# Two attention pairs project keys and queries in split form, and raw inputs share two buffers

## The chip, the cores and the metric

The kernel runs on one core of one Trainium2 chip. The metric is the device time of one execution in microseconds. A profiled execution is recorded by the hardware profiler; its trace gives every instruction with its start and duration.

## The reference

Three stages run one after the other, all in float32.

- Linear attention for 4 batches of 8 heads, 576 positions, head size 64. For queries and keys, `proj = x @ w_phi` (64 to 128 features), the row's largest absolute value is taken off, and the features are `[exp(proj), exp(-proj)]`. Then `kv = k_p^T v`, `z = sum(k_p)`, and the output is `(q_p kv) / (q_p z + 1e-6)`.
- A maxout layer on 2304 tokens: `h = max(x w1, x w2, x w3)`, 512 to 768, followed by `h @ w_out` back to 512.
- A layer with learned slopes: `h = x w_in` (512 to 2048), `g = max(h, 0) + alpha * min(h, 0)`, then `g @ w_out`.

## The kernel before

**Pairs.** Heads are taken in pairs, 16 in all (4 batches of 4 pairs), numbered here from 0. A pair's 576 positions are four tiles of 128 and a tail of 64; the tails of its keys and its queries share one fifth tile. So each pair has nine projections of one tile: four of keys, four of queries, one of tails. `project` (line 204) does two tiles in one PSUM bank of tag `pj`, which has two buffers; VectorE then reduces the bank to row maxima (line 212) and, for most uses, adds them back (`less_max`, line 216).

**Two forms of a product.** In the plain form a projection is one float32 matmul of 128x256. In the split form `features` (line 192) makes two reduced-width halves of the raw tile on VectorE, a cast (line 67, tiles `xh..`) and a subtraction (line 70, tiles `xl..`), and three matmuls of 128x256 take the products high by high, high by low and low by high, with the weights' halves `wph` and `wpl`. Pairs 0 to 4 are plain (`PLAIN = 5`), pairs 5 to 15 are split. The halves of keys and queries have two buffers of tag `xh` and two of tag `xl`.

**Loads.** `load_pair` (line 140) loads keys `k`, tails `t`, queries `q` and values `v` on SyncE's queue. In plain pairs the raw keys lie in the two buffers of tag `xh` and the raw queries in the two of `xl`. In split pairs raw keys and raw queries take turns in two buffers of tag `raw`. The tails have one buffer.

**The loop** (line 453). For pair i it emits the loads of pair i+1, then `queries` of pair i-1 interleaved with `keys` of pair i, then the conversion of some weight tiles of the maxout layer (`CONVERT_IN`, of lowest priority), and from pair 5 on some units of the maxout layer (`layer1`), which are other TensorE work beside the attention. The halves `wph` and `wpl` are emitted just before the keys of pair 4.

**What sets the order.** The code is written as above, but a planner with a model of the engines' times sorts each engine's instructions, and the loads of SyncE's queue, by priority and by when their inputs and buffers are ready. The order is then fixed: each engine and each queue goes through its list in order, and waits on semaphores. The keys of batch 0 have neutral priority; queries of the pair before have a slightly lower one, weight conversions a still lower one.

Of the kernel before, what the change touches and what calls it, by code (L numbers as in the profile page):

```python
# [38 lines left out]
XBUFS = 6  # L39
LAG = 2  # L40
KEYS_ONLY = ("rv", "rt", "vh", "vl", "e", "kh", "kl", "my", "begun", "xht", "xlt")
PLAIN = 5
CONVERT_IN = (0, 1, 1, 2, 2, 3, 4, 5)
SOON, NOW, LATER, LAST = 400, 1000, -100, -200

# [2 lines left out]
def tile_kernel(ctx: ExitStack, tc: tile.TileContext, qT, kT, tails, v, w_phi, w1, w2, w3, w_out, w_in, w_out2, alpha, out):  # L48
# [14 lines left out]
    def hi_act(dst, src):  # L63
        A.activation(dst, src, AF.Copy)  # L64

    def hi_dve(dst, src):
        V.tensor_copy(dst, src)

    def sub(eng, dst, src, hi):
        eng.tensor_tensor(dst, src, hi.bitcast(F32), op=ALU.subtract)  # L70
# [18 lines left out]
    def run(*steps):  # L89

        steps = list(steps)
        while steps:
            for x in list(steps):
                if next(x, x) is x:
                    steps.remove(x)
# [13 lines left out]
    def bank(tag, bufs, nm):  # L109
        return ps.tile([P, 512], F32, tag=tag, bufs=bufs, name=nm)  # L110
# [8 lines left out]
    def at(shape, dtype, name, tag=None, bufs=1):  # L119
        pool = ap if (tag or name) in KEYS_ONLY else lp  # L120
        return pool.tile(shape, dtype, name=name, tag=tag or name, bufs=bufs)
# [18 lines left out]
    def load_pair(pair):  # L140

        odd = pair[1] % 2
        tags = ["xh", "rv", "rt", "xl"] if plain(pair) else ["raw", "rv", "rt", "raw"]
        if plain_kv(pair):
            tags[1] = ("vl", "vh")[odd]
        shapes = ([P, SM], [P, 5, 3, D], [P, 2 * ST], [P, SM])
        for what, tag, shape, src in sorted(zip("kvtq", tags, shapes, (kT, v, tails, qT)), key=lambda x: ("ktqv" if i_of(pair) else "ktvq").index(x[0])):
            t = at(shape, F32, tag=tag, bufs=2 if tag in ("raw", "xh", "xl") else 1, name=what)
            for part in (slice(0, 2 * P), slice(2 * P, SM)) if what == "k" and i_of(pair) == 0 else (slice(None),):
                nc.sync.dma_start(t[:, part], src[pair][:, part])  # L150
            raws[pair, what] = t

    def plain(pair):
        return i_of(pair) < PLAIN

    def i_of(pair):
        return pair[0] * NPAIR + pair[1]

    def plain_kv(pair):
        return pair[0] < 2  # L160

    def split_w123(f, j):
        if j == 0:
            w.append([])
        t = ring.tile([P, 2, 512], F32R, tag="w", name="w123t")
        w[f].append(t)
        st = fetched.pop(0)
        wt = at([P, 512], F32, tag="kl", bufs=2, name="wt")
        yield from from_f64(st, wt, tc.keep_in_program_order, False)
        hi_act(t[:, 0], wt)  # L170
        yield
        sub(V, t[:, 1], wt, t[:, 0])
# [3 lines left out]
    def fetch(after):  # L176

        tag = ("kh", "qe")[len(unfetched) % 2]
        st = at([P, 1024], U32, tag=tag, bufs=2, name="wst")
        V.tensor_copy(st[:, :1].bitcast(F32), after[:, :1])  # L180
        nc.sync.dma_start(st, unfetched.pop(0).bitcast(U32))
        fetched.append(st)

    def at_priority(n, steps):
        while True:
            with tc.high_priority(offset=n):
                x = next(steps, steps)
            if x is steps:
                return
            yield  # L190
# [76 lines left out]
    def keys(pair):  # L267

        rv = raws[pair, "v"]
        if not plain_kv(pair):  # L270
            if not vs:
                vs.extend(at([P, 5, 3, D], F32R, tag=tag, bufs=1, name=tag) for tag in ("vh", "vl"))
                part = slice(None)
            else:
                part = slice(None, None, 2)
            vh, vl = vs
            hi_act(vh[:, :, part], rv[:, :, part])
            sub(V, vl[:, :, part], rv[:, :, part], vh[:, :, part])
        kvp = bank("kv", 1, "kvp")
        first = True  # L280
        for tiles, e in exp_keys(pair):
            n = len(tiles) * 512
            if not plain_kv(pair):
                kh = at([P, 1024], F32R, tag="kh", bufs=2, name="kh")
                kl = at([P, 1024], F32R, tag="kl", bufs=2, name="kl")
                hi_act(kh[:, :n], e[:, :n])
                sub(V, kl[:, :n], e[:, :n], kh[:, :n])
                ops = ((vh, kh), (vl, kh), (vh, kl))
            yield
            for i, t in enumerate(tiles if plain_kv(pair) else ()):  # L290
                for j in range(4):
                    c = slice(i * 512 + j * P, i * 512 + j * P + P)
                    nc.tensor.matmul(  # L293
                        kvp[:, j * P : (j + 1) * P],
                        e[:, c],
                        rv[:, t, j // 2 : j // 2 + 2].rearrange("p a d -> p (a d)"),
                        start=first,
                        stop=t == 4,
                        skip_group_check=True,
                    )  # L300
                    first = False
            for i, t in enumerate(() if plain_kv(pair) else tiles):
                for h in range(2):
                    c = slice(i * 512 + h * 256, i * 512 + h * 256 + 256)
                    for x, y in ops:
                        nc.tensor.matmul(  # L306
                            kvp[:, h * 256 : h * 256 + 256],
                            x[:, t, h : h + 2].rearrange("p a d -> p (a d)"),
                            y[:, c],
                            start=first,  # L310
                            stop=t == 4 and y is ops[-1][1],
                            skip_group_check=True,
                        )
                        first = False
        yield
        if plain_kv(pair):
            kvf = at([P, 2, 2, P], F32, tag=("kvh", "kvl")[pair[1] % 2], bufs=2, name="kvf")
            A.activation(kvf.rearrange("p a b c -> p (a b c)"), kvp, AF.Copy)  # L318
            kvs_of[pair] = (kvf,)
            return  # L320
        kvs = at([P, 512], F32, tag="kvs", bufs=1, name="kvs")
        A.activation(kvs, kvp, AF.Copy)
        kvt = bank("kv", 1, "kvt")
        for i in range(4):
            nc.tensor.transpose(kvt[:, i * P : (i + 1) * P], kvs[:, i * P : (i + 1) * P], ident)
        kvh = at([P, 2, 2, P], F32R, tag="kvh", bufs=2, name="kvh")
        kvl = at([P, 2, 2, P], F32R, tag="kvl", bufs=2, name="kvl")
        hi_act(kvh.rearrange("p a b c -> p (a b c)"), kvt)
        sub(V, kvl.rearrange("p a b c -> p (a b c)"), kvt, kvh.rearrange("p a b c -> p (a b c)"))
        kvs_of[pair] = (kvh, kvl)  # L330
# [114 lines left out]
    w = []  # L445

    load_pair(pairs[0])
    make_identity(nc, ident)
    al = const.tile([P, NF2], F32, name="al")
    nc.gpsimd.dma_start(al, alpha)  # L450
    G.tensor_scalar(al, al, -1.0, 1.0, op0=ALU.mult, op1=ALU.add)
    last = None
    for i, pair in enumerate(pairs):
        if i + 1 < len(pairs):
            load_pair(pairs[i + 1])
        with tc.high_priority(offset=(0, SOON, NOW, NOW)[pair[0]]):
            if i == PLAIN - 1:
                hi_dve(wph, wraw)
                sub(V, wpl, wraw, wph)
            run(*([at_priority(LATER, queries(last))] if last else []), keys(pair))  # L460
            last = pair
        count = CONVERT_IN[i] if i < len(CONVERT_IN) else 0
        for j in range(count):
            for _ in range(min(count, 4) if j == 0 else int(j + 3 < count)):
                fetch(begun[pair])
            with tc.high_priority(offset=LAST if i < NPAIR - 1 else 0):
                n = sum(len(x) for x in w)
                run(split_w123(n // 3, n % 3))
        u0 = 3 * (i - NPAIR) - LAG
        for u in range(u0, u0 + 3):  # L470
            if u >= 0:
                c, f = (u % 2, u // 2) if u < 12 else (u // NF1 % 2, u % NF1)
                layer1(u // 12, c, f, xs[u // 12], w[f])
# [369 lines left out]
    for block in range(nblocks):  # L843
        last = block == nblocks - 1
# [97 lines left out]
```

## Time and profile before

| what | us |
|---|---|
| median of 3 runs (lowest, highest) | 877.71 (877.59, 879.58) |
| the profiled execution's own time | 878.6 |
| its span, first to last instruction | 876.8 |
| TensorE matmuls busy | 868.5 |
| TensorE weight loads busy | 854.9 |
| VectorE busy | 637.3 |
| ScalarE busy | 514.5 |
| GpSimd busy | 158.4 |

Matmuls are pipelined, so the time between the ends of two of them, not the duration of one, is what one costs. Weight loads lie beside matmuls. Idle time of an engine that is not the bottleneck costs nothing.

### The profile page before, as it was taken

To read this page: it belongs to the slowest core of one execution; us is meant where nothing else is said; L and a number is where in the kernel's file an instruction comes from. 1 tells how busy PE (TensorE), PEld (TensorE's weight loads), DVE (VectorE), ACT (ScalarE), POOL (GpSimd) and SP (SyncE) were. 2 spreads that over 40 slices of the span, in tenths; PEclk is the share of its full clock that TensorE was granted. 3 is DMA by queue.
4 is the path that set the end of the run, shared out by engine and by line. 5 is a ranking of instruction groups with operands and counts; after the bars stand their busy time and mean duration, and the time that the engine had idled before them with its cause. 6 is when DMAs were issued, how large, how long until landed. Compare 5 with 4: busy or idle time off the path is not lost.

```text
span 876.8 us, 17441 instructions
## 1 busy us (share of the span) xinstructions
PE 868.5 (99%) x6631; PEld 854.9 (97%) x6631; DVE 637.3 (73%) x1196; ACT 514.5 (59%) x1055; POOL 158.4 (18%) x278
## 2 busy tenths in 40 slices
PE   9999999999999999999999999999999999999998
PEld 8888899999999999999999999999999999999998
DVE  5578878877888776683965754846478899988871
ACT  4666767777677765553853554646477763544440
POOL 0354222112322244211112301111111000000000
PEclk9999999999999999999999999999999999999999
DMA  6445653223332169661688863745348746433321
GB/s 234 140 157 161 180 154 113 76 86 85 88 89 70 36 215 349 212 208 35 195 266 309 314 230 134 225 182 189 123 136 265 268 158 202 150 125 121 120 74 49
DMA packets 70436, 142.99 MB, mean 163 GB/s; under 512 B 9152, under 2 KB 36176, under 8 KB 70352
## 3 DMA queue, kind: packets, MB, share of 16 engines
q1 hardware_dynamic: 53664, 92.95, 33.2%
q0 software_dynamic: 14816, 45.26, 15.0%
q10 hardware_dynamic: 1872, 3.67, 1.2%
q8 instruction: 52, 0.85, 0.4%
q14 instruction: 32, 0.26, 0.1%
HBM read 93.07 MB, written 46.34 MB: 159 GB/s over the span
## 4 chain that ended last, share of the span: by engine, by line
PE 82%; issue 8%; DMA 4%; ACT 3%; DVE 2%; POOL 1%; POOLq 0%; DVEq 0%; ACTq 0%
PE acc L861 20%; PE p L265 16%; PE sums L773 12%; PE pj L265 6%; PE pc L773 6%; PE pn L265 6%; PE kvp L293 4%; PE p L675 3%; PE kvp L306 3%; PE pb L773 3%; DMA st<-in_w_out 2%; PE pt L368 2%; DMA xr<-r_d 1%; DVE wt L86 1%; DMA st<-in_w_in 1%
## 5 line engine op out<-in xcount | busy, mean ns | idle before, releaser
L265 PE MATMUL p<-x,w123t 128*128 128x288 f32 x1728 | 251.4, 298 | 0.4 <-ACT s L436 0.4
L265 PEld LDWEIGHTS p<-x,w123t 128*128 128x128 f32 x1728 | 235.0, 188 | 2.3 <-ACT s L436 0.8
L773 PE MATMUL sums<-x,wi 128*128 128x288 f32 x768 | 107.7, 295 | 0.0
L861 PE MATMUL acc<-wq,o 128*128 128x256 f32 x864 | 105.5, 283 | 0.0
L861 PEld LDWEIGHTS acc<-wq,o 128*128 128x128 f32 x864 | 104.2, 189 | 0.0
L773 PEld LDWEIGHTS sums<-x,wi 128*128 128x128 f32 x768 | 104.0, 188 | 0.0
L861 PE MATMUL acc<-wq,x 128*128 128x256 f32 x648 | 78.1, 280 | 0.0
L675 PE MATMUL p<-x,wo 128*128 128x288 f32 x576 | 77.0, 296 | 0.6 <-ACT yo L679 0.6
L675 PEld LDWEIGHTS p<-x,wo 128*128 128x128 f32 x576 | 76.6, 188 | 0.9 <-ACT yo L679 0.8
L861 PEld LDWEIGHTS acc<-wq,x 128*128 128x128 f32 x648 | 77.0, 188 | 0.0
L792 DVE SCALAR_TENSOR_TENSOR g<-neg,al,g 128x576 f32<-128x576 f32 x64 | 50.3, 811 | 23.6 <-ACT neg L791 23.6
L212 DVE TENSOR_REDUCE mx<-pj 128x4 f32<-128x512 f32 (+1 forms) x80 | 50.1, 628 | 12.3 <-PE pj L265 12.2
L781 ACT ACTIVATE s<-sums 128x576 f32<-128x576 f32 x48 | 31.1, 647 | 42.0 <-PE sums L773 41.9
L77 ACT ACTIVATE wt<-st 128x512 f16<-128x512 bf16 x38 | 30.1, 799 | 42.5 <-DVE wt L514 14.0
L793 POOL DMA_DIRECT2D g_d<-g x32 | 22.9, 715 | 167.2 <-DVE g L792 165.4
L441 POOL DMA_DIRECT2D h_d<-ho x48 | 28.2, 587 | 137.8 <-DVE ho L439 116.3
L245 ACT ACTIVATE ke<-pj,mx 128x128 f32<-128x128 f32 x96 | 36.9, 384 | 14.7 <-DVE mx L212 14.5
L293 PEld LDWEIGHTS kvp<-v,ke 128*128 128x128 f32 x320 | 40.6, 191 | 4.7 <-ACT kvf L318 1.8
L293 PE MATMUL kvp<-v,ke 128*128 128x128 f32 x320 | 42.9, 278 | 1.6 <-ACT kvf L318 1.6
L791 ACT ACTIVATE neg<-g 128x576 f32<-128x576 f32 x64 | 40.2, 675 | 6.3 <-DVE g L823 5.9
L64 ACT ACTIVATE o<-wt 128x512 fp32r<-128x512 f32 x45 | 27.4, 627 | 24.7 <-PE acc L861 14.2
L400 POOL DMA_DIRECT2D xr<-r_d x64 | 34.1, 539 | 32.3 <-DMA r_d<-dc 21.6
(161 smaller groups left out, 1779.6 us busy)
## 6 DMA issues: line engine op xcount, KB each, us to landing
g_d<-g POOLq DMA_DIRECT2D x32, 576.0 KB, 3.6
a<-g_d SPq DMA_DIRECT2D x36, 512.0 KB, 4.3
st<-in_w_out SPq DMA_DIRECT2D x22, 512.0 KB, 5.8
wst<-in_w SPq DMA_DIRECT2D x18, 512.0 KB, 4.0
st<-in_w_in SPq DMA_DIRECT2D x16, 512.0 KB, 4.7
yr<-y_d SPq DMA_DIRECT2D x28, 288.0 KB, 3.9
v<-in_v SPq DMA_DIRECT2D x16, 480.0 KB, 4.4
q_d<-wt POOLq DMA_DIRECT2D x28, 256.0 KB, 5.3
```

The lines of the kernel that those rows point to most:

```text
L77: order(A.activation(half[:, :, 1].bitcast(F16), lanes[:, :, 3].bitcast(BF16), AF.Copy))
L212: V.tensor_reduce(mx, pv, axis=AX.X, op=ALU.max, apply_absolute_value=True, negate=True)
L245: A.activation(ev[:, a, 0], pv[:, a], AF.Exp, bias=mx[:, a : a + 1])
L265: nc.tensor.matmul(dst, x, y, start=i == 0, stop=i == len(ops) - 1, **kw)
L293: nc.tensor.matmul(kvp[:, j * P : (j + 1) * P], e[:, c], rv[:, t, j // 2 : j // 2 + 2].rearrange("p a d -> p (a d)"), start=first, stop=t ...
L400: nc.gpsimd.dma_start(xr[r], rows[h : h + 1, cs].to_broadcast([D, CH]))
L675: nc.tensor.matmul(p2[m // 2][1][:, m % 2], x, y, start=k + n == 0, stop=k == NF1 - 1 and n == 2)
L773: nc.tensor.matmul(dst[:, j], a, b, start=start and n == 0, stop=n == len(ops) - 1, skip_group_check=True)
L781: A.activation(s, src, AF.Copy)
L791: A.activation(neg, gv[:, j], AF.Relu, scale=-1.0)
L792: V.scalar_tensor_tensor(gv[:, j], neg, al[:, f + j : f + j + 1], gv[:, j], op0=ALU.mult, op1=ALU.add)
L861: nc.tensor.matmul(acc[i], x, y, start=half == 0 and f == 0 and n == 0 and place[i][1] == 0, stop=half == 1 and f == 3 and n == 2, skip_gr ...
```

## The change

Plain are now pairs 0, 3 and 4 alone; pairs 1 and 2 use the split form. The raw keys and queries of every pair but the first lie in the two buffers of tag `raw`, also those of the plain pairs 3 and 4, which therefore keep such a buffer until their last projection has read it. The halves of the weights are emitted after the keys of pair 0.

```diff
-PLAIN = 5
+PLAIN = (0, 3, 4)
...
     def load_pair(pair):
 
         odd = pair[1] % 2
-        tags = ["xh", "rv", "rt", "xl"] if plain(pair) else ["raw", "rv", "rt", "raw"]
+        tags = ["xh", "rv", "rt", "xl"] if i_of(pair) == 0 else ["raw", "rv", "rt", "raw"]
...
     def plain(pair):
-        return i_of(pair) < PLAIN
+        return i_of(pair) in PLAIN
...
         with tc.high_priority(offset=(0, SOON, NOW, NOW)[pair[0]]):
-            if i == PLAIN - 1:
+            run(*([at_priority(LATER, queries(last))] if last else []), keys(pair))
+            if i == 0:
                 hi_dve(wph, wraw)
                 sub(V, wpl, wraw, wph)
-            run(*([at_priority(LATER, queries(last))] if last else []), keys(pair))
             last = pair
```

## Rows read from the trace of the kernel before

**Rows 1.** The page, part 1: engine, busy us (share of span), instructions
```profile
PE 868.5 (99%) x6631; PEld 854.9 (97%) x6631; DVE 637.3 (73%) x1196; ACT 514.5 (59%) x1055; POOL 158.4 (18%) x278
```
**Rows 2.** Busy time by stretch: stretch, its length, busy us (instructions), granted clock, DMA
```profile
3.70:11.28 7.58, 6.97 (x34) 5.46 (x34) 4.21 (x10) 3.13 (x6) 0.20 (x1) 1.00 0.97 339
11.28:24.01 12.73, 12.73 (x92) 11.96 (x91) 8.11 (x15) 6.48 (x16) 0.00 (x0) 1.00 0.51 173
24.01:37.34 13.33, 13.33 (x86) 11.93 (x85) 8.33 (x18) 8.24 (x19) 2.77 (x6) 1.00 0.41 133
51.11:64.57 13.46, 13.46 (x87) 12.00 (x85) 8.56 (x20) 9.26 (x29) 8.63 (x14) 1.00 0.55 174
64.57:80.00 15.43, 15.43 (x107) 14.17 (x105) 15.43 (x33) 11.29 (x32) 8.58 (x14) 1.00 0.57 184
80.00:95.00 15.00, 12.92 (x93) 11.44 (x92) 11.08 (x28) 11.24 (x32) 4.21 (x8) 1.00 0.53 150
```
**Rows 3.** Waits of TensorE, whole span: who waited for whom, us, times, longest
```profile
PE kvp L293 <- ACT kvf L318: 1.6, 1, 1.6
PE pn L265 <- ACT q L376: 0.5, 1, 0.5
```
**Rows 4.** Chain of waits in order of time: start, us, what
```profile
15.20 1.73 PE pj L265 x8
92.28 0.72 PE pj L265 x6
```
**Rows 5.** The tile pj: instructions that write it, min/median/max ns, first and last start
```profile
L265 PEld LDWEIGHTS pj<-wph,xhk x44: 186/188/192, 64.5 to 294.8; 128*128 128x128 f32 x44
L265 PE MATMUL pj<-wraw,k x40: 379/379/792, 3.7 to 57.0; 128*128 128x256 f32 x40
```
**Rows 6.** VectorE in order of time: start, us, instruction [idle before <-releaser]
```profile
4.01 0.43 DVE L70 TENSOR_TENSOR wpl<-wraw,wph 128x256 fp32r<-128x256 f32 x1
5.81 0.69 DVE L212 TENSOR_REDUCE mx<-pj 128x4 f32<-128x512 f32 x1 [1.38 <-PE pj L265]
45.16 0.41 DVE L67 CAST xhk<-k 128x512 fp32r<-128x512 f32 x1
60.13 0.41 DVE L67 CAST xhq<-q 128x512 fp32r<-128x512 f32 x1
64.94 0.22 DVE L67 CAST xht<-t 128x128 fp32r<-128x128 f32 x1
65.84 0.27 DVE L70 TENSOR_TENSOR xlt<-t,xht 128x128 fp32r<-128x128 f32 x1
72.85 1.69 DVE L70 TENSOR_TENSOR xlq<-q,xhq 128x512 fp32r<-128x512 f32 x1
```
**Rows 7.** The tile xlk, 0 to 130 us: its subtraction on VectorE
```profile
L70 DVE TENSOR_TENSOR xlk<-k,xhk x4: 672/680/693, 56.3 to 119.3; 128x512 fp32r<-128x512 f32 x4
```
**Rows 8.** SyncE's queue in order of time: start, us of the issue, load
```profile
4.49 0.66 SPq L150 DMA_DIRECT2D k<-in_kT  x1
5.20 0.50 SPq L150 DMA_DIRECT2D q<-in_qT  x1
57.02 0.33 SPq L150 DMA_DIRECT2D k<-in_kT  x1
61.93 4.54 SPq L150 DMA_DIRECT2D t<-in_tails  x2
```
**Rows 9.** DMA issues, 57.0 to 57.3 us: KB, us from issue to landing
```profile
k<-in_kT SPq DMA_DIRECT2D x1, 256.0 KB, 4.7
```
**Rows 10.** TensorE in order of time: start, us, matmuls
```profile
56.32 1.03 PE L265 MATMUL pj<-wraw,k 128*128 128x256 f32 x4
64.57 0.47 PE L265 MATMUL pj<-wph,xhk 128*128 128x256 f32 x1
69.83 1.03 PE L265 MATMUL pj<-wraw,q 128*128 128x256 f32 x4
80.68 0.36 PE L265 MATMUL pj<-wph,xhq 128*128 128x256 f32 x1
```

## Prediction

> **What bounds the kernel now.** The engine shares come first: TensorE is busy for 868.5 of the span's 876.8 us [rows 1]. Then the busy time by stretch, for the part that the change touches (pairs 1 and 2 lie between about 11 and 37 us): TensorE is busy without a gap in 11.28 to 24.01 and 24.01 to 37.34, while VectorE is busy 8.11 of 12.73 and 8.33 of 13.33 us, and the granted clock is 1.00 throughout, the 2.4 GHz level [rows 2]. No other TensorE work fills this part, only attention. Third, TensorE's waits: after the start two matter, 1.6 and 0.5 us, both in the stretch 80 to 95, where 2.08 of 15.00 us are idle [rows 2, 3]. So a microsecond of TensorE work taken out between 11 and 37 us should come out of the time, as long as VectorE, which gets new work, and the loads keep up.
>
> **1. TensorE: three cheap matmuls for one dear one.** The 40 records of plain key products stand for 5 pairs of 4 tiles, so one plain product is two records [rows 5]. In the chain eight records take 1.73 us, so a product costs 1.73 / 4 = 0.433. In split form six matmuls, two products, take 0.72, with rounding 0.357 a product by the ends of its records (three times 0.119) [rows 4]. The saving is 0.076 on each of 9 products in 2 pairs: 18 x 0.076 = 1.37 us. Bounds: 1.3 with 0.360 a product, 1.4 with 0.355.
>
> The durations of the records (379 ns plain) overlap and are no price [rows 5].
>
> Against this step stands the Trainium skill, "Perfetto Trace Analysis", section "Identifying the Most-Contended Engine": how near TensorE is to its limit is to be judged by the weight loads' busy share, not by that of the matmuls. By that meter the change adds work, since three loads replace two. What time that gives is the fourth rival below; this case's rows speak against it, as three loads of 0.188 us pass in 0.357.
>
> **2. VectorE: casts and subtractions.** Each of the two pairs gains a cast of keys and one of queries (0.41 each), two subtractions (0.68 each, the median of xlk), and for the tails 0.22 and 0.27: 2 x 1.09 + 0.49 = 2.67 us a pair, 5.3 in all [rows 6, 7]. In these stretches VectorE idles for 4.62 and 5.00 us [rows 2]. With TensorE's part shortened by 0.69 a pair, 11.0 of about 12.6 us would be busy. The raw tiles lie ready early (the loads are a pair ahead), so the new instructions can be done in the gaps, and I count them at 0. The cover isn't complete: VectorE works in order, and a reduction that arrives behind a subtraction is up to 0.68 late. Behind it wait the row sums, the exponentials and the matmuls of keys by values. Bounds: 0 to 5.3 us, all of it on the path. I take the lower end because VectorE stays under its limit in throughput; it was full, 15.43 of 15.43, in the stretch from 64.57 with TensorE also full, though there with other TensorE work beside it [rows 2].
>
> **3. The weights' halves.** They were already done by 4.44 us, in a gap before the first reduction at 5.81, although their line stands at pair 4 [rows 6]. Their new place in the program, after the keys of pair 0, is still earlier than where they were, and that gap of 1.38 us stays. Cost 0; moved behind the first reductions, at most 0.72 (0.29 and 0.43).
>
> **4. The loads, in SyncE's queue.** Keys and queries of pair 5, the first in the raw buffers, were loaded at 4.49 and 5.20 us [rows 8], when the DMA engines were 97% busy [rows 2]. Now these buffers hold pairs 1 to 4 first. Two loads leave the crowded start; TensorE's only gap there (7.58 less 6.97) is not theirs, so this counts 0, at best 0.61.
>
> The later loads are chained: each takes the buffer of the pair before. For pairs 2 and 3 the buffer is free as soon as a subtraction is done, most of a pair ahead, so 0. The tightest is the key load of pair 5. It waits for the last key projection of pair 4, before at 56.32 + 1.03 = 57.35, after 1.37 us earlier, 55.98. Landing takes 4.7 [rows 9], so 60.68; cast and subtraction 1.09 more, 61.77. The first projection that needs it stood at 64.57 [rows 10], now 63.20, so 1.43 us are to spare and I take 0. The upper bound is the second rival. The query load of pair 5 waits for the last query projection of pair 4 (69.83 + 1.03 - 1.37 = 69.49), lands at 74.2, and its halves are done at 75.3, against a need at 80.68 - 1.37 = 79.31 [rows 10].
>
> That last shift has a price. The cast of pair 5's queries stood at 60.13, in a stretch where VectorE had room (8.56 of 13.46); now it comes at about 74, in the stretch 64.57 to 80 in which VectorE is full [rows 2, 6]. The subtraction was already there, at 72.85. In a full stretch 0.41 us pushes everything behind it, and among this is what leads to the waits at 80 to 95. I count +0.41, with bounds of 0 and 1.09 (if the subtraction comes late too).
>
> **Sum.** -1.37 + 0 + 0 + 0 + 0.41 = -0.96 us. The profiled execution's own time is 878.6 (span 876.8 and 1.8 around it), so it would become 877.6 with a span of 875.8. It lies 0.9 above the median of the runs, 877.71; taken from the median the forecast is 876.75.
>
> **The rivals.**
>
> *First, faster: the waits at 80 to 95 go too.* They hang on a chain of small transfers of batch 0's last pair, which all start 1.37 us earlier. If the planner's new order brings that chain ahead of the TensorE work that waits, the 2.08 idle us go: 877.71 - 1.37 - 2.08 = 874.3. For it: the two waits are single events, which any other order may miss [rows 3]. Against it: everything moves by the same amount, and VectorE is full just before.
>
> *Second, slower: the key load of pair 5 comes late.* SyncE's queue keeps its order. If this load is put behind the tails of the same pair, which were issued at 61.93 [rows 8] and wait for the tail projection of pair 4, it starts at 60.56, lands at 65.26 and is split at 66.35, 3.15 us after its projection could start; and 1.09 us of VectorE work falls into the full stretch. 876.75 + 3.15 + 1.09 = 881.0. It decides from an issue after 63.20 - 1.09 - 4.7 = 57.4 on. For it: the tails' single buffer. Against it: the planner put the keys of pair 6 at 57.02, ahead of those tails, in the kernel before [rows 8].
>
> *Third, slower: VectorE becomes the pace of pairs 1 and 2.* If each of the three reductions of keys and tails in two pairs finds a subtraction of 0.68 ahead and nothing else fills TensorE: 6 x 0.68 = 4.1, so 876.75 + 4.1 = 880.8. For it: 11.0 of 12.6 busy, and no other work for TensorE. Against it: idle VectorE time of about 1.6 us a pair remains.
>
> *Fourth, slower: weight loads set the pace.* If three loads of 0.188 took turns, a split product would take 0.564 in place of 0.433: 18 x 0.131 = +2.36, with 0.41 gives 880.5. The chain's six split matmuls in 0.72 us speak against it [rows 4, 5].
>
> *Fifth, the change does not do what it says:* the TensorE time is saved and comes back as short waits of the same size in pairs 1 to 5, and only the moved cast remains: 877.71 + 0.41 = 878.1.
>
> **How the numbers follow.** Forecast 0.50, first 0.17, second 0.08, third 0.14, fourth 0.03, fifth 0.08. What a measurement of this kernel can tell from no change is about 0.3%, 2.6 us: below 875.1 is faster, above 880.3 slower. Faster holds the first rival and a little of the forecast's own spread, 0.21. Slower holds the second and fourth and most of the third, some of which is smaller than its full price, 0.20. Within 0.3%: 0.59. The forecast's own range, from its bounds in steps 1 to 4 with short waits of up to 1.5 us, is 875.6 to 878.6. The range to hold it 8 times in 10 goes down to the first rival, 874.2, and up to 880.4, which leaves out the second and half of the third.
>
> **What would show it.** Step 1: split products of pairs 1 and 2 at 0.12 us a matmul, and TensorE's work up to the first projection of pair 5 earlier by about 1.4 us. Step 2: no new TensorE waits between 11 and 37 us, VectorE busy about 11 us a pair. Step 3: the weights' halves still before 5.81. Step 4: keys of pair 5 issued near 56 and split before 63; the wait of 2 us at 80 to 95 still there, somewhat longer. Wrong would be a key load behind the tails, waits of TensorE for row sums or exponentials, or a changed order of the whole later plan, whose idle time is small now and has more room to grow than to shrink.

## The result, and the profile after

The changed kernel takes 883.12 us (median of 6; 881.94 to 884.39) against 877.65 (877.26 to 879.58) on the same chip: a ratio of 1.0052 [1.0037, 1.0067]. It is slower, by 4.6 us by the ratio and 5.5 by the medians, and outside the range that was forecast. The profiled execution took 882.35, which is 3.75 more than that of before (878.6); its span is 880.5 (876.8). The mean granted clock over the whole span was 0.998, 0.998, 0.996, 0.998, 0.998 and 1.000 in the six executions of after; in the profiled one of before it is 1.000.

The page, part 1, and the tile pj of the kernel after (instructions that write it, min/median/max ns, first and last start us):

```profile
PE 868.6 (99%) x6649; PEld 856.0 (97%) x6649; DVE 643.5 (73%) x1208; ACT 513.4 (58%) x1055; POOL 158.2 (18%) x278
```
```profile
L265 PE MATMUL pj<-wraw,k x24: 378/379/797, 3.8 to 57.0; 128*128 128x256 f32 x24
L265 PE MATMUL pj<-wph,xhk x52: 277/283/522, 12.6 to 292.4; 128*128 128x256 f32 x52
```

The change does what it says: 24 plain records in place of 40 [rows 5], and split products from 12.6 us on, where before they began at 64.5. VectorE is busy 6.2 us longer than before, near the 5.3 of the new casts and subtractions. TensorE's busy time did not fall (868.6 and 868.5 [rows 1]), as work at a lower clock, shown below, lasts longer, and its idle time, span less busy, grew from 8.3 to 11.9.

Where the idle time is, by stretch (length, busy us of PE, PEld, DVE, ACT and POOL with instructions, granted clock, DMA), after:

```profile
3.70:11.28 7.58, 6.53 (x27) 4.76 (x26) 4.57 (x10) 1.15 (x2) 0.19 (x1) 1.00 0.90 308
11.28:24.01 12.73, 12.47 (x95) 12.04 (x96) 10.26 (x24) 7.36 (x17) 0.00 (x0) 1.00 0.43 151
24.01:37.34 13.33, 13.33 (x101) 12.49 (x101) 9.18 (x22) 9.22 (x21) 2.32 (x5) 1.00 0.40 113
37.34:51.11 13.77, 13.61 (x90) 12.04 (x89) 8.68 (x18) 8.26 (x20) 8.14 (x14) 1.00 0.55 169
51.11:64.57 13.46, 12.81 (x81) 11.33 (x81) 10.71 (x21) 9.29 (x28) 8.17 (x14) 1.00 0.61 193
64.57:80.00 15.43, 13.73 (x94) 12.20 (x93) 13.84 (x32) 9.96 (x28) 8.04 (x13) 1.00 0.58 177
80.00:95.00 15.00, 14.18 (x103) 12.93 (x103) 10.61 (x28) 11.10 (x33) 4.21 (x8) 1.00 0.52 172
340.00:350.00 10.00, 7.88 (x52) 7.42 (x51) 4.62 (x10) 5.46 (x10) 2.15 (x4) 0.91 0.81 273
350.00:360.00 10.00, 10.00 (x71) 10.00 (x71) 5.97 (x15) 4.60 (x8) 1.68 (x4) 0.92 0.75 238
```

and three stretches of before that [rows 2] does not hold:

```profile
37.34:51.11 13.77, 13.74 (x86) 11.95 (x85) 8.77 (x20) 7.83 (x19) 7.89 (x14) 1.00 0.53 170
340.00:350.00 10.00, 10.00 (x77) 10.00 (x77) 5.21 (x12) 4.38 (x7) 4.54 (x9) 1.00 0.99 370
350.00:360.00 10.00, 9.97 (x73) 9.58 (x73) 6.25 (x15) 7.13 (x12) 1.11 (x2) 1.00 0.74 243
```

Length less TensorE's busy time is what to read. From 3.70 to 95 before idles 2.72 us (0.61 at the start, 0.03, and 2.08 at 80 to 95), after 4.64 (1.05, 0.26, 0.16, 0.65, 1.70, 0.82): 1.92 more, against 1.37 saved, so about +0.5. This is a low count, since the ends of matmuls are modelled: the first maxout product, `p` below, starts at 68.5 in after and at 67.5 in before with the same products ahead of it, so after is 1.0 late there. From 95 to 120 after idles 0.68 us more (14.40 busy of 15.00 and 9.92 of 10.00; before is full). From 340 to 360 after idles 2.12 us, and its granted clock is 0.91 and 0.92, so (0.09 + 0.08) x 10 = 1.7 us of full clock are missing; before has 0.03 and 1.00. That is +3.8, far behind the part that was changed. These sum to more than the profiled 3.75: from 360 to 690 before idles 1.0 us (79.61 busy of 80.00 and 249.39 of 250.00) and after is full.

TensorE's waits over the whole span, after (us in total, times, longest):

```profile
PE pj L265 <- ACT ke L246: 1.9, 2, 1.5
PE p L265 <- ACT nd L357: 1.8, 1, 1.8
```

With the 1.09 us at 11.54 below, put down to "issue", these are the three places. **At the start** VectorE's list now has the cast of pair 1's keys ahead of the second reduction of pair 0 (in order of time; in brackets the idle time before and what ended it):

```profile
8.87 0.43 DVE L67 CAST xhk<-k 128x512 fp32r<-128x512 f32 x1 [1.49 <-DMA k<-in_kT]
9.21 0.68 DVE L212 TENSOR_REDUCE mx<-pj 128x4 f32<-128x512 f32 x1
17.37 0.69 DVE L70 TENSOR_TENSOR xlq<-q,xhq 128x512 fp32r<-128x512 f32 x1 [1.76 <-PE pj L265]
```

and the same reduction before, directly after the work that started at 6.61:

```profile
7.21 0.68 DVE L212 TENSOR_REDUCE mx<-pj 128x4 f32<-128x512 f32 x1
```

The cast waits 1.49 us for its load; the reduction behind it starts at 9.21, 2.0 later than before. Until a reduction and what follows it are done, the product's buffer isn't free. The subtraction at 17.37 waits again: its buffer of tag `xl` still held raw queries of pair 0. TensorE, after:

```profile
11.54 1.10 PE L265 MATMUL pj<-wraw,q 128*128 128x256 f32 x4 [1.09 <-issue]
12.61 0.36 PE L265 MATMUL pj<-wph,xhk 128*128 128x256 f32 x1
22.64 0.28 PE L265 MATMUL pj<-wph,xlq 128*128 128x256 f32 x1
22.76 0.28 PE L265 MATMUL pj<-wph,xhq 128*128 128x256 f32 x1
51.15 1.03 PE L265 MATMUL pj<-wraw,k 128*128 128x256 f32 x4
74.77 0.39 PE L265 MATMUL pj<-wph,xhk 128*128 128x256 f32 x1 [1.54 <-ACT ke L246]
```

The first row is that wait. "issue" means that the profile shows no releaser; the experiment f2 below shows which it was. The two at 22.64 and 22.76 are 0.12 us apart, the forecast price of a split matmul. The first key projections of pair 1 and of pair 4 before:

```profile
11.28 1.03 PE L265 MATMUL pj<-wraw,k 128*128 128x256 f32 x4
51.11 1.03 PE L265 MATMUL pj<-wraw,k 128*128 128x256 f32 x4
```

From pair 1 to pair 4 TensorE does the same products in both, but for the 18 in the other form. After takes 51.15 - 12.61 = 38.54 us for them, before 39.83: 1.29 less, near the 1.37. But pair 1 started 12.61 - 11.28 = 1.33 late, which eats it up.

**At pair 5** the same thing happens again. SyncE's queue, and then VectorE, after:

```profile
57.42 0.33 SPq L150 DMA_DIRECT2D k<-in_kT  x1
66.34 0.33 SPq L150 DMA_DIRECT2D q<-in_qT  x1
```
```profile
65.62 0.69 DVE L70 TENSOR_TENSOR xlk<-k,xhk 128x512 fp32r<-128x512 f32 x1
70.23 0.43 DVE L67 CAST xhq<-q 128x512 fp32r<-128x512 f32 x1 [1.45 <-DMA q<-in_qT]
70.69 1.17 DVE L70 TENSOR_TENSOR xlq<-q,xhq 128x512 fp32r<-128x512 f32 x1
71.78 0.68 DVE L212 TENSOR_REDUCE mx<-pj 128x4 f32<-128x512 f32 x1
```

Pair 5's queries took the raw buffer that the subtraction of its keys had just left (65.62 + 0.69 = 66.31), were issued at 66.34 and landed at 70.23, 3.9 later. Their cast stands for 1.45 us with a reduction behind it, and the exponentials behind that reduction are what TensorE waits for until 74.77.

**At 340 to 350** the engine that stands is ScalarE. After:

```profile
341.94 0.80 ACT L77 ACTIVATE wt<-st 128x512 f16<-128x512 bf16 x1 [1.55 <-DMA xr<-r_d]
346.37 0.78 ACT L77 ACTIVATE wt<-st 128x512 f16<-128x512 bf16 x1 [2.93 <-DMA st<-in_w_out]
347.02 0.40 ACT L357 ACTIVATE nd<-pn 128x320 f32<-128x320 f32 x1
```

and the same engine before:

```profile
340.30 0.44 ACT L357 ACTIVATE nd<-pn 128x320 f32<-128x320 f32 x1 [0.44 <-PE pn L265]
```

Two conversions of later weights, before which the engine stood 1.55 and 2.93 us, the second time for its load, come ahead of the copy `nd`, which frees a bank that TensorE needs: idle for 1.79 us until 347.48. From 348.2 the granted clock is at the lower level, 1.2 GHz, for some 3.4 us. Before, the copy came first.

Landmarks in TensorE's order show that nothing more is lost later. The tiles p and acc (last start us at the end of a range), before:

```profile
L265 PE MATMUL p<-x,w123t x1728: 288/295/537, 67.5 to 437.4; 128*128 128x288 f32 x192
L861 PE MATMUL acc<-wq,o x864: 277/283/287, 687.3 to 873.0; 128*128 128x256 f32 x173
```

and after:

```profile
L265 PE MATMUL p<-x,w123t x1728: 289/295/607, 68.5 to 442.2; 128*128 128x288 f32 x192
L861 PE MATMUL acc<-wq,o x864: 276/283/288, 691.1 to 876.8; 128*128 128x256 f32 x173
```

After is 4.8 behind when the first maxout products end (442.2 and 437.4), and 3.8 both where the last stage starts and where it ends.

### The profile page after: what moved, and what is told of

It is laid out like the page before. It is cut to its first block, busy times and chain, and to the rows that moved or that the text cites. A ratio compares the mean times of both kernels' runs of the same rounds, so it can differ in the third digit from the quotient of the medians.

```text
span 880.5 us, 17503 instructions
## 1 busy us (share of the span) xinstructions
PE 868.6 (99%) x6649; PEld 856.0 (97%) x6649; DVE 643.5 (73%) x1208; ACT 513.4 (58%) x1055; POOL 158.2 (18%) x278
## 4 chain that ended last, share of the span: by engine, by line
PE 60%; DMA 2%; DVE 0%; ACT 0%; issue 0%; ACTq 0%; SPq 0%; DVEq 0%
PE acc L861 20%; PE sums L773 12%; PE p L265 11%; PE p L675 9%; PE pc L773 6%; PE pb L773 3%; DMA st<-in_w_out 2%; DVE wt L86 0%; DVE x L70 0%; ACT wt L77 0%; ACT st L80 0%; DVE out L873 0%; ACT s L436 0%; ACT nd L357 0%; DVE wt L84 0%
```

## The experiments

Every kernel was compared with the kernel before on the same chip, where that one's median was between 877.07 and 877.46.

### First round: which part of the change costs

**e1_raw_only**: the kernel before with the new buffers alone (pairs 0 to 4 plain).

```diff
-        tags = ["xh", "rv", "rt", "xl"] if plain(pair) else ["raw", "rv", "rt", "raw"]
+        tags = ["xh", "rv", "rt", "xl"] if i_of(pair) == 0 else ["raw", "rv", "rt", "raw"]
```

> The kernel before, pairs 0 to 4 still plain, with only the raw tiles of pairs 1 to 15 in two buffers. Theory (three separate losses: the start, the loads in pairs 3 to 5, a late wait at 345 us): no loss at the start against the kernel before (TensorE's first 24 us lose 2.5 us in both), TensorE waits of 0.5 to 1.5 us more between 51 and 95 us, so 878.2 to 879.2 if the late wait isn't there. Rival (the loss is the added VectorE work of the split form alone): 877.7, as before, with no new waits before 110 us.

Measured: 886.98, ratio 1.0107 [1.0079, 1.0136], worse than the whole change. The losses lie at other places than forecast: from 51 to 95 us TensorE idles 2.21, hardly more than before (2.08), but it idles 1.93 of 10 us at 100 to 110 and 2.30 at 345 to 355, where the clock is 0.84. The theory that the buffers cost little was wrong; that they cost a fixed part of the whole loss can't be read from it either, as its order is neither that of before nor that of after.

**e2_four_raw**: the change with four raw buffers in place of two.

```diff
-            t = at(shape, F32, tag=tag, bufs=2 if tag in ("raw", "xh", "xl") else 1, name=what)
+            t = at(shape, F32, tag=tag, bufs=4 if tag == "raw" else 2 if tag in ("xh", "xl") else 1, name=what)
```

> The changed kernel with four raw buffers in place of two, so that keys and queries are two deep again. Theory: the start still loses 1.3 us more than before, since VectorE's order there has nothing to do with the buffers; the waits between 51 and 80 us (2.35 us in the changed kernel) fall below 1 us; about 881.5 if the late wait stays, 878 if the new plan misses it. Rival (VectorE's added work makes these waits): waits between 51 and 80 us stay near 2.3 us.

Measured: 881.71, 1.0056 [1.0034, 1.0078]. The cure works where it was aimed: TensorE is busy 15.43 of 15.43 us at 64.57 to 80, and by chance 340 to 350 is full too; but 80 to 95 idles 2.33 us (after 0.82). Its profiled execution is its fastest, 879.63. The median is still not better than that of the change.

**e4_pn_last**: the change with another order of three banks in the spread units of the maxout layer, aimed at the late wait.

```diff
-                p = bank(("pn", "pt", "kv")[j], 1, "p1")
+                p = bank(("kv", "pt", "pn")[j], 1, "p1")
```

> The changed kernel, where the spread units of the maxout layer use the bank of tag pn last and that of kv first; every other engine's order is unchanged. Theory (the wait at 345 us is for that bank, which ScalarE frees late, and the half clock after it follows from the wait): no wait of 1.8 us there and no stretch of half clock, 2.3 to 3.4 us less than the changed kernel, 879.7 to 880.8. Rival (TensorE is held there by the weight loads in any case): it waits as long for another bank or for the maxima behind it, 883.

Measured: 882.85, 1.0065 [1.0039, 1.009]. The theory fell: the late wait moved instead of going, and the one at pair 5 grew, although the plan there is the same as after. Its waits, and VectorE and GpSimd beside each other:

```profile
PE pj L265 <- ACT ke L246: 4.2, 1, 4.2
PE p L265 <- ACT s L436: 3.1, 1, 3.1
```
```profile
68.16 2.40 DVE L67 CAST xhq<-q 128x512 fp32r<-128x512 f32 x1 [0.69 <-DMA q<-in_qT]
70.59 2.56 DVE L70 TENSOR_TENSOR xlq<-q,xhq 128x512 fp32r<-128x512 f32 x1
```
```profile
68.06 1.55 POOL L402 TENSOR_TENSOR xr<-nd,xr 128x288 f32<-128x288 f32 x2
```

The load landed 2 us earlier than in after, so the cast started at 68.16 in place of 70.23, beside GpSimd's work, and took 2.40 in place of 0.43, the subtraction 2.56 in place of 1.17.

**e6_pair2_only**: the change with only pair 2 newly split.

```diff
-PLAIN = (0, 3, 4)
+PLAIN = (0, 1, 3, 4)
```

> The changed kernel with pair 1 plain again, so that only pair 2 is split. Theory (at the start VectorE's casts of pair 1 stand ahead of reductions of pair 0 and wait for a key load): the loss of 1.3 us in the first 24 us is gone, the saving is 0.7 in place of 1.4 us, so 882.4 with the late wait, 879 without. Rival (the start loses by its crowded loads, whatever is split): the first projection of pair 1 still stands 1.3 us later than before.

Measured: 882.2, 1.0056 [1.0035, 1.0077]. The start is cured (TensorE busy 7.55 of 7.58 us), so the wait there belongs to the split form of pair 1. But 2.06 us are lost at 24.01 to 37.34, where VectorE waits 1.97 us for pair 2's queries and after that for weights.

### Second round: cures of the two early waits

**f2_after_gate**: the change, with a copy of one column that makes pair 1's casts come after pair 0's reductions.

```diff
+        if i_of(pair) == 1 and what != "t":
+            V.tensor_copy(xh[:, :1], tail_of[pairs[0]][:, 0, :1])
         hi_dve(xh, x)
```

> The changed kernel with one more VectorE instruction ahead of each cast of pair 1, which reads a column of pair 0's last tail result, so that the two casts stand behind all of pair 0's reductions in VectorE's list. Theory (VectorE works in order, and a cast that waits for its load holds up the reductions behind it): the changed kernel's loss of 4.0 us in the first 24 us falls to 2.6 to 2.9, as before. The rest of the plan is a new one, so the time is 881.5 if the later losses stay. Rival (the start loses because the loads are crowded): the first key projection of pair 1 stays at 12.6 us.

Measured: 879.87, 1.0028 [1.0018, 1.0039], about half of the loss. TensorE in f2:

```profile
10.48 1.03 PE L267 MATMUL pj<-wraw,q 128*128 128x256 f32 x4
```

No wait is before it, and 3.70 to 11.28 is busy for 7.58 us. So the wait put down to "issue" came from the casts ahead of the reductions. Pair 1's first split product is not earlier for it: it starts at 13.05 (after 12.61), with other products now ahead of it. From 11.28 to 24.01 0.40 us of idle are left (after 0.26). Its time from 340 to 360 differs too (idle 2.21, clock 1.00), so not all of the gain is the start's.

**f1_four_raw_gate**: f2 and e2 together.

```diff
+            t = at(shape, F32, tag=tag, bufs=4 if tag == "raw" else 2 if tag in ("xh", "xl") else 1, name=what)
...
+        if i_of(pair) == 1 and what != "t":
+            V.tensor_copy(xh[:, :1], tail_of[pairs[0]][:, 0, :1])
```

> Both cures: four raw buffers and pair 1's casts behind pair 0's reductions; pairs 1 and 2 split. Theory: both waits of VectorE for a load go, what is left is the 1.37 us that the split form saves and the luck of the later plan: 876 to 879. Rival (split pairs cost VectorE time that TensorE has no cover for): 881 or more, with waits of TensorE for VectorE or ScalarE between 12 and 60 us.

Measured: 883.41, 1.007 [1.0054, 1.0086]. The first 20 us are perfect (busy 20.31 of 20.31 from 3.70 to 24.01), and the time is lost later: 1.90 of 10 us idle at 110 to 120, then a clock of 0.83; 1.63 at 340 to 350, then 0.86. Four raw buffers, which work where they are put, make f2 slower (1.0070 in place of 1.0028). The rival's time came true, but not its waits: from 12 to 60 us TensorE is almost full.

**f5_raw_only_four**: e1 with four raw buffers.

```diff
+        tags = ["xh", "rv", "rt", "xl"] if i_of(pair) == 0 else ["raw", "rv", "rt", "raw"]
...
+            t = at(shape, F32, tag=tag, bufs=4 if tag == "raw" else 2 if tag in ("xh", "xl") else 1, name=what)
```

> All of pairs 0 to 4 plain, as before, raw tiles of pairs 1 to 15 in tag raw as in the changed kernel, but with four buffers. Theory (two buffers make the loads late, which gave 887 with two): 877 to 879. Rival (what cost 10 us with two buffers is only another order of the later plan): 880 or more, as the order is again a new one.

Measured: 885.11, 1.0082 [1.0061, 1.0104]. The two intervals overlap, so the scarcity of raw buffers is not most of what costs in e1. VectorE and TensorE in f5:

```profile
45.77 0.89 DVE L84 TENSOR_SCALAR wt<-wst 128x512 uint16<-128x512 uint16 x1 [5.66 <-DMA wst<-in_w]
```
```profile
48.86 0.67 PE L265 MATMUL pj<-wraw,t 128*128 128x256 f32 x2 [1.44 <-issue]
```

A weight conversion of the lowest priority stands 5.66 us for its load, with two reductions behind it.

**f3_four_raw_gate_all**: f1 with every pair but the first split.

```diff
-PLAIN = (0, 3, 4)
+PLAIN = (0,)
```

> Both cures and pairs 1 to 4 split, only pair 0 plain. Theory: TensorE saves 2.7 us in place of 1.37, VectorE gains 5.3 us more in pairs 3 and 4, where it also converts two weight tiles a pair: 875 to 879. Rival (VectorE has no room in pairs 3 and 4): new TensorE waits of 2 us or more between 37 and 80 us, 880 or more.

Measured: 883.44, 1.0057 [1.0034, 1.008]. The rival came true: with twice the saving, TensorE waits four times for the subtractions `pp` on VectorE, 4.6 us in all, and idles 2.24 of 13.77 at 37.34 to 51.11.

### Third round: how much a new order alone is worth

These three change the order and nothing of weight: a copy of one column (0.15 us) on VectorE in pair 3 or pair 6 of the kernel before, into a tile that takes one turn in the four buffers of tag `mx`, and other low priorities in the kernel before.

**n2_spare3** and **n2_spare6** (with 6 in place of 3):

```diff
-            pv, mx = project(ops, tiles)
+            pv, mx = project(ops, tiles); (i_of(pair), g) == (3, 0) and V.tensor_copy(at([P, 4], F32, tag="mx", bufs=4, name="spare")[:, :1], mx[:, :1])
```

> The kernel before with one more VectorE instruction: a copy of one column (0.15 us) in the keys of pair 3, which nobody reads. It makes the planner order all engines anew from there on. Theory A (the time of this kernel hangs on the planner's order, and the order before is a good draw): 3 to 8 us slower than before, though the work is the same. Theory B (the changed kernel is slower by what it does: late loads and casts ahead of reductions): as before, 877 to 878.

> The same copy in the keys of pair 6, so that the order is the one of before up to there and a new one from about 75 us on. Theory A: slower by 2 to 8 us, all of it behind 75 us. Theory B: 877 to 878.

Measured: 878.39, 1.0011 [0.9994, 1.0029], and 881.34, 1.0048 [1.0031, 1.0065]. The first can't be told from before; the second is clearly slower. In n2_spare6 (VectorE, then TensorE):

```profile
116.71 0.17 DVE L390 TENSOR_SCALAR dc<-dc 128x9 f32<-128x9 f32 x1 [4.11 <-DMA dc<-nd]
```
```profile
120.13 0.49 PE L293 MATMUL kvp<-v,ke 128*128 128x128 f32 x2 [1.70 <-ACT ke L245]
```

A copy of 0.15 us costs 4.2 us by the ratio. It is the pattern of after again: an engine stands for a transfer, here 4.11 us, what TensorE needs is behind it, TensorE idles 1.70 us, and the clock at 120 to 130 is 0.83.

**n4_later**: the kernel before with

```diff
-SOON, NOW, LATER, LAST = 400, 1000, -100, -200
+SOON, NOW, LATER, LAST = 400, 1000, -150, -250
```

> The kernel before with slightly lower priorities of queries and weight conversions (-150 and -250 in place of -100 and -200), no other work. Theory A: slower by 2 to 8 us. Theory B: 877 to 878.

Measured: 879.58, 1.0027 [1.0009, 1.0045]. For the kernel before this order is a little worse.

**a_later**: the change with the same line as n4_later. Up to 199.6 us TensorE's order is that of after; from there it is another.

> The changed kernel with the same lower priorities: another order of the same work from about 130 us on, the same start. Theory A: between 878 and 888, not near the changed kernel in particular; the wait at 345 us may go. Theory B: 883, as the changed kernel, since its late loads and casts are the same.

Measured: 878.29, 1.0008 [0.9993, 1.0024]. The same change, with TensorE's order the same for the first 200 us, is now within measurement of before; theory B, 883, fell. The mean granted clock is 0.999 or 1.000 in all of its twelve executions, where after had 0.996 to 0.998 in five of six. A stretch, ScalarE and the tile p in a_later:

```profile
340.00:350.00 10.00, 10.00 (x77) 10.00 (x76) 6.13 (x14) 5.86 (x10) 5.40 (x9) 1.00 0.98 368
```
```profile
341.94 0.43 ACT L357 ACTIVATE nd<-pn 128x320 f32<-128x320 f32 x1
```
```profile
L265 PE MATMUL p<-x,w123t x1728: 288/295/542, 67.5 to 438.7; 128*128 128x288 f32 x192
```

The copy comes at 341.94, five microseconds earlier than after; TensorE is full and at full clock; the end of the maxout products is at 438.7 (before 437.4, after 442.2). Of the change's loss, 0.0052 - 0.0008, 3.9 us by the ratios and 4.8 by the medians, is the order after 200 us; by the two intervals the 3.9 is uncertain by some 2 us. The late stall of after is the part of it that a trace shows. The page of a_later, span 877.0, part 1:

```profile
PE 866.8 (99%) x6649; PEld 854.8 (97%) x6649; DVE 641.0 (73%) x1208; ACT 514.8 (59%) x1055; POOL 157.6 (18%) x278
```

TensorE is busy 1.7 us less than before and idle for 10.2 in place of 8.3: the saving is there, and waits take it back.

### Fourth round: the cures in this order

**c2_four_later**, **c1_four_gate_later**, **c3_gate_later**, **c5_pair2_later**: e2, f1, f2 and e6, each with

```diff
-SOON, NOW, LATER, LAST = 400, 1000, -100, -200
+SOON, NOW, LATER, LAST = 400, 1000, -150, -250
```

> The changed kernel with four raw buffers and the lower priorities of queries and conversions. What the changed kernel does early is cured in part (loads), its late order is another draw. Theory (start 1.4 us worse, mid waits as before, 1.37 saved, late wait missed): 876.5 to 878.5. Rival (the late loss comes back in any order but that of before): 880 or more.

> The same with pair 1's casts behind pair 0's reductions as well. Theory: start as before, so 875 to 877, below the kernel before. Rival: 880 or more, with waits at places that the earlier runs did not show.

> The changed kernel (two raw buffers) with pair 1's casts behind pair 0's reductions and the lower priorities. Theory: waits for the query load of pair 5 stay (1.5 to 2.5 us between 64 and 80 us), the late wait is missed: 877 to 879. Rival: 880 or more.

> The changed kernel with only pair 2 split (pair 1 plain) and the lower priorities. Theory: its early loss of 2.4 us between 24 and 37 us stays, 0.7 saved, late wait missed: 878 to 880. Rival: 882, as with the other priorities.

Measured: c2 882.14, 1.0053 [1.0033, 1.0073]; c1 883.81, 1.0077 [1.0054, 1.01]; c3 876.98, 1.0002 [0.9991, 1.0013]; c5 880.0, 1.0041 [1.0027, 1.0054]. c2 and c1 missed their expectations, and their rivals' 880 or more came true; c3 and c5 came out about as expected. The line that took 4 us off the change takes 2.3 off f2 and nothing off e2 and f1: no setting is good in itself, each kernel gets another order from it. c3 is the best version of the change, and within measurement equal to the kernel before. Stretches in c3:

```profile
3.70:11.28 7.58, 7.37 (x34) 5.77 (x34) 5.17 (x13) 3.15 (x6) 0.20 (x1) 1.00 0.87 310
340.00:350.00 10.00, 10.00 (x77) 10.00 (x77) 5.52 (x11) 6.38 (x10) 1.23 (x3) 1.00 0.79 260
```

Both the start and the late stretch are as good there as before.

## Why the prediction was wrong

**The sum had no term for the new plan.** The failed step is the sum itself: it carries four terms over an order taken as fixed, and names "a changed order of the whole later plan, whose idle time is small now and has more room to grow than to shrink" only among the signs at the end, with no price and no chance. The runs put there: 3.9 us of the 4.6 for after against a_later, and +0.0011, +0.0048 and +0.0027 for three reorders of the kernel before that change nothing of weight. None of the three is faster, and two are slower beyond their intervals. So before seems to be not at a typical order but at a good one, with 8.3 us idle in 876.8, and a change that makes the planner sort anew gives up that good order; three reorders are few to show this. A term of +1 to +4 us from such an argument, with the larger part of the chances, would have been nearer than -0.96.

**Step 1 was right.** A split matmul costs 0.12 us, and from pair 1 to pair 4 TensorE took 1.29 us less. But none of it had arrived when pair 4's first key projection began, 51.15, before 51.11, since pair 1 had begun 1.33 late.

**Step 2 failed too.** It counted VectorE's new work at 0; at the start that work cost 1.33. VectorE kept room: busy 10.26 of 12.73 and 9.18 of 13.33 us, below the forecast 11 a pair. What failed is "the raw tiles lie ready early". Pair 1's keys landed at 8.87, while the planner had put their cast ahead of a reduction that could have started near 7.2. The forecast bounded the lateness by a subtraction's 0.68; the row shows 2.0, since what stands ahead of the reduction is a wait for a load. 1.09 us of it shows as TensorE's wait, and f2 takes that wait away.

**Step 3 was right.** The halves of the weights were done at 4.53, before the first reduction at 5.91, as forecast, and cost nothing.

**Step 4 was half right.** The keys of pair 5 were issued at 57.42 instead of near 56, just where the second rival would begin to decide (57.4), and split only at 66.31 instead of before 63. But they did not stand behind the tails, and TensorE, which reached their first projection at 67.52 with other work ahead of it, did not wait for them, so the second rival did not happen. It was the queries that came late: not in the buffer of pair 4's queries, as I had them, but in the one that pair 5's keys had left. They landed before the forecast 74.2, but their cast had been put earlier still, and the 0.41 us of its work became a stand of 1.45 us, with 1.54 of TensorE's idle behind it.

**The rivals.** The first, that the waits at 80 to 95 go, came true in part (idle 0.82 in place of 2.08), against the forecast's "somewhat longer"; it was outweighed. The second and third came nearest in time, 881.0 and 880.8; the second did not happen, and the third's cause is only partly there: reductions were late, but behind waits and not behind the throughput of subtractions. The fourth is refuted by the pitch of 0.12. The fifth, that the saving comes back as short waits in pairs 1 to 5, is about what the early part did, but its 878.1 holds nothing for the late order.

**What stays open.** The sign of the early part alone: a_later lies between -0.6 and +2.1 us (0.9993 to 1.0024), and c3, without the wait at the start, between -0.8 and +1.1. Single executions differ as much: `p` begins at 68.5 in after and at 67.5, as in before, in a_later, which has the same order up to there. Why new buffers alone (e1, f5: 1.0107 and 1.0082) lose more than any of the three neutral reorders: order and loads were not separated there. And e2's profile shows neither the wait of pair 5 nor the late one, yet its median is no better than that of after; where its other executions lose, no trace shows.

## What to carry to other kernels

Where a planner fixes each engine's order, a change of less than its reorders are worth (here up to 0.5%) can't be predicted by adding up the work: price the new order as a term of its own, here as a loss, as the plan was already nearly full, and before blaming the change compare it with neutral reorders. For each instruction added to an engine that works in order, ask when its load lands against when the work behind it is needed; a free engine helps nothing if it stands at a wait. A cure that removes a wait early in the kernel is a new order for all that follows, so judge it by the time, not by the wait.

## What the runs showed of the hardware

The same cast of 128x512 on VectorE took 0.43 us in after and 2.40 in e4, and the same subtraction 0.69 at 17.37, where GpSimd does nothing, and 2.56 in e4 (1.69 in before [rows 6]); the two in e4 lie beside GpSimd's own tensor work. The Trainium skill, "SBUF — State Buffer", section "Who interferes with whom", says that a VectorE instruction with two SBUF inputs, or one in a mode that uses two ports, contends with a GpSimd instruction that reads SBUF, and that whichever issues first shuts the other out for the whole instruction. The trace agrees in kind: 2.40 and 2.56 beside GpSimd's tensor work from 68.06 on. So 2 us of difference between two executions of one plan can come from a load that lands 2 us earlier.

TensorE's granted clock fell to 1.2 GHz for some microseconds behind an idle time of 1.79 us in after, 1.70 in n2_spare6 and 4.16 in e4, but not behind 1.54 at pair 5 in after, 1.57 in before (the 1.6 of [rows 3]) or 2.15 in a_later:

```profile
74.37 0.39 PE L265 MATMUL pj<-wph,xhk 128*128 128x256 f32 x1 [2.15 <-ACT ke L246]
```

There the stretch 64.57 to 80 has a clock of 1.00. So in these traces the length of one stall does not tell whether the clock falls. Where it fell, in after, the 1.79 us cost 1.7 us of full clock more.
